# Score matmuls on 32-column tiles of the PE array, and 56 KB rows in the first two zero fills

## The chip, the cores and the metric

The kernel runs on one core of a Trainium2 chip. The metric is the device time of one execution in microseconds; for the kernel before, three timed runs gave 766.21, 766.40 and 766.55 us, median 766.4 us. Profiles come from one more execution, taken by the hardware profiler; its times are counted from the start of its span.

## The reference

A decode step with its gradients. Two tokens (B = 2, width D = 512) are layer-normalised; one branch is attention over the last 4,096 positions of a key and a value cache of 32,768 positions (8 KV heads of 128, 4 query heads each), the other is a two-layer squared-ReLU network whose output goes through silu and gates the first. The outputs are the result and the gradients of all inputs, the two caches among them.

```python
def _A_ref(x, k_cache, v_cache, wq, wo):
    W = min(4096, max(256, Sk // 4))
    k = jnp.repeat(k_cache[:, :, Sk - W:, :], rep, axis=1)
    v = jnp.repeat(v_cache[:, :, Sk - W:, :], rep, axis=1)
    scores = jnp.einsum("bhqd,bhkd->bhqk", q, k) * (Dh ** -0.5)
    p = _softmax(scores, axis=-1)
    o = jnp.einsum("bhqk,bhkd->bhqd", p, v)
    return ... @ wo
xn = _layernorm(x, axis=-1)
s = _A_ref(xn, A_k_cache, A_v_cache, A_wq, A_wo)
g = _silu(_B_ref(xn, B_w1, B_b1, B_w2, B_b2))
return x + s * g
_out, _vjp = jax.vjp(_f, A_x, A_k_cache, A_v_cache, A_wq, A_wo, B_w1, B_b1, B_w2, B_b2)
_grads = _vjp(grad_out)
```

The cache gradients, `out_2` (keys) and `out_3` (values), have the shape of the caches, 134 MB each in bf16. All but the last 4,096 of the 32,768 positions are zero, because the forward pass doesn't read them: 28,672 rows for each of 16 (batch, head) pairs of each cache have to be written with zeros, 7.34 MB (the profile's 7,168 KB) each and 234.9 MB in all.

## The kernel before

**Zero fills.** `zt` is a tile of zero bytes, 14,336 for each of 128 partitions (L80). `zf` (L90) issues a DMA from it to a stretch of `out_2` or `out_3` on the GpSimd queue (POOL); the 31 fills `qi` = 0 to 30 (L118 to L123) are issued one after the other at the head of the program, as far as the queue takes them. Fills in `zlong` (L107) are one DMA with 128 rows of 224 positions, 57,344 bytes (56 KB) each; fills in `zshort` (L108) are several DMAs with rows of up to 28 KB; the others, 0 and 1 among them, are one DMA with 2 x 128 rows of 112 positions, 28,672 bytes (28 KB) each. A row of 56 KB is written from the same 14,336 bytes of `zt`, which the DMA widens from bytes to 32-bit words (L96); the 28 KB rows are widened from bytes to bf16. The 32nd fill is the last DMA of SyncE's queue (SP), L641: it is issued after the store of `out_6` (L636) and after the fill before the last one on POOL has landed (L642).

**Loads.** SP's queue loads `w1`, `w2`, `wo`, `wq` and the first value block at once (L229 to L233). x, the incoming gradient and the two biases come on ScalarE's queue (ACT, L222 to L228); the bias `b2` is the last of these, and VectorE (DVE) converts it (L246) before anything else of the forward pass.

**Rounds.** Attention works in four rounds `r` (L430) of one batch and four KV heads. Heads are `NP` = 4 blocks of `RB` = 32 rows in every score tile of 128 x 512 in PSUM: row pr * 32 + g * 4 + i is head pr, position group g (of 8), query i (of 4). A round has a value block `vnat` and a key block `knat` of 128 x 16,384 bf16 (4,096 KB each). `scores` (L378) is called twice, for dP = dO V^T (`dp_ps`, from `vnat`) and S = Q K^T (`s_ps`, from `knat`). For each of 16 groups (2 halves x 8 g) it makes 8 transposes of 128 x 128 on TensorE (PE, L384) into one of two PSUM tiles `tp`, copies the result to one of four places of `tring` (three times on DVE, once on ACT, L387), and adds four matmuls (L391), one for each head, into `out_ps`. The stationary operand of these is a window of 128 columns in `zz`: zeros but for the 4 columns in which the queries of this head stand, so that each matmul adds zeros to the rows of all other heads and groups. Then come the softmax (L438 to L452), `contract` (L394) and `outer_store` (L412), which overwrites the block with its gradient and stores it on ACT's queue (L422). The next round's block is loaded on SP into the same buffer (L543, L550), which waits for that store.

**The end.** The last round holds the rest of the backward pass. Three rows of small results, `out_rows` (L499), `db2r` (L507) and `du_rows` (L515), are put into `zz`, which is no longer needed by then. After the rounds come the weight gradients: `out_4` from `wq` and `out_5` from `wo` on ACT's queue (L581, L587), `out_8` from `w2T` and `out_6` from `dw` on SP's (L610, L636), then the last fill.

The order of the instructions on each engine is set by a list scheduler with its own cost model; semaphores are set by dependences between tiles.

Of the kernel before, what the change touches and what calls it, by code (L numbers as in the profile page):

```python
# [11 lines left out]
BF16 = mybir.dt.bfloat16  # L12
# [4 lines left out]
def kernel(  # L17
# [24 lines left out]
    nc = tc.nc  # L42
    P = 128
    B, _, D = A_x.shape
# [3 lines left out]
    REP = HQ // HKV  # L48
# [5 lines left out]
    G = 8  # L54
    NP = 4
    PB = P // NP
    NCB = W // PB
    CC = NCB // G
    CH = 8
    NH = CC // CH  # L60
    RB = G * REP
    R = NP * RB
# [41 lines left out]
    ZQ = 2 * B * HKV  # L104
    zparts = [(out_2, q) for q in range(B * HKV)] + [(out_3, q) for q in range(B * HKV)]

    zlong = (3, 5, 7, 11, 12, 16, 17, 18, 19, 22, 23, 24, 25, 26, 27, 28, 29, 30)  # L107
    zshort = {  # L108
        2: ((5, 8, 2), (120, 68, 3), (128, 32, 1), (16, 1, 1)),
        4: ((3, 1, 2), (2, 99, 6), (128, 112, 1), (128, 102, 1), (86, 1, 1)),  # L110
# [60 lines left out]
    def pk_rows(t):  # L171
        return t.rearrange("b (p k) -> b k p", k=DK)
# [17 lines left out]
    nc.vector.tensor_scalar(out=nsel[:], in0=sel[:], scalar1=1e30, scalar2=-1e30, op0=ALU.mult, op1=ALU.add)  # L190
    pperm = const.tile([P, NP, PB], BF16, name="pperm")
    nc.vector.tensor_copy(out=pperm[:], in_=ident_bf[:].rearrange("p (k b) -> p b k", b=NP))
    ZO = R - REP
    ZW = NP * (ZO + R)
    zz = const.tile([P, 2 * ZW], BF16, name="zz")
    nc.vector.memset(zz[:], 0.0)
    zq = zz[:, 0:ZW].rearrange("p (n w) -> p n w", n=NP)
    zdo = zz[:, ZW:2 * ZW].rearrange("p (n w) -> p n w", n=NP)
    p_bf = const.tile([R, CC, PB, NP], BF16, name="p_bf")
# [20 lines left out]
    with tc.tile_pool(name="pw", bufs=1) as pw:  # L220
# [44 lines left out]
        for fk in range(FK):  # L265
            for k in range(DK):
                nc.tensor.matmul(hps[:, fk, :], lhsT=w1[:, k, fk:F:FK], rhs=xnT[:, k, :],
                                 start=(k == 0), stop=(k == DK - 1))
# [6 lines left out]
        for dk in range(DK):  # L275
            for fk in range(FK):
                nc.tensor.matmul(ups[:, dk, :], lhsT=w2[:, fk, dk:D:DK], rhs=h2T_bf[:, fk, :],
                                 start=(fk == 0), stop=(fk == FK - 1))
# [23 lines left out]
        for j0 in range(0, NJ, JG):  # L302
# [8 lines left out]
            for dk in range(DK):  # L311
                nc.tensor.matmul(dops[0:B, :, :], lhsT=dsT_bf[:, dk, :], rhs=woT[:, :, dk, :],
                                 start=(dk == 0), stop=(dk == DK - 1))
# [7 lines left out]
        for n0 in range(0, N, 512):  # L321
            qps = ps_o.tile([P, 512], F32, tag="o")
            for k in range(DK):
                nc.tensor.matmul(qps[0:B, :], lhsT=xnT[:, k, :], rhs=wq[:, k, n0:n0 + 512],
                                 start=(k == 0), stop=(k == DK - 1))
# [29 lines left out]
    small = attn.enter_context(tc.tile_pool(name="small", bufs=1))  # L355
    one = attn.enter_context(tc.tile_pool(name="one", bufs=1))
    epi = attn.enter_context(tc.tile_pool(name="epi", bufs=1))

    def group_sum(out_t, src, op, mask, comb, negate=False):
        tmp = small.tile([R, RB], F32, tag="gs")  # L360
        nc.vector.tensor_scalar(out=tmp[:], in0=mask[:].rearrange("p g i -> p (g i)"), scalar1=src[:, 0:1],
                                scalar2=None, op0=comb)
        nc.vector.tensor_reduce(out=out_t[:], in_=tmp[:], axis=AX.X, op=op, apply_transpose=True, negate=negate)
# [14 lines left out]
    def scores(out_ps, nat, zbuf):  # L378
        n = 0
        for half in range(NH):  # L380
            for g in range(G):
                tp = ps_t.tile([P, CH, P], BF16, tag="pt")
                for j in range(CH):
                    nc.tensor.transpose(tp[:, j, :], nat[:, g * CC + half * CH + j, :], pperm[:].rearrange("p b k -> p (b k)"))  # L384
                tF = tring[:, n % 4 * CH * R:(n % 4 + 1) * CH * R]
                tT = tF.rearrange("p (c b k) -> p c b k", c=CH, b=NP)
                evac(tF, tp[:].rearrange("p c k -> p (c k)"), eng=("act" if n % 4 == 3 else "dve"))  # L387
                n += 1
                for pr in range(NP):
                    o = ZO - (pr * RB + REP * g)  # L390
                    nc.tensor.matmul(out_ps[:, half * CH * PB:(half + 1) * CH * PB], lhsT=zbuf[:, pr, o:o + R], rhs=tT[:, :, pr, :],  # L391
                                     start=(g == 0 and pr == 0), stop=(g == G - 1 and pr == NP - 1))

    def contract(src, nat):  # L394
        cols = []
# [34 lines left out]
    for r in range(NR):  # L430
        nc.vector.tensor_copy(out=zdo[:, :, ZO:ZO + REP], in_=heads(doT_all, r))
        nc.vector.tensor_copy(out=zq[:, :, ZO:ZO + REP], in_=heads(qT_all, r))

# [33 lines left out]
        if r == NR - 1:  # L467
            o_rows = tring[0:B, 0:N]
            for h0 in range(0, HQ, 8):
                tp = ps_t.tile([B, 8, P], BF16, tag="pt")  # L470
                for h in range(8):
                    nc.tensor.transpose(tp[:, h, :], oT_all[:, h0 + h, :], ident_bf[:, :])
                evac(o_rows[:, h0 * DH:(h0 + 8) * DH], tp[:].rearrange("b h p -> b (h p)"))
            tp = ps_s.tile([P, NJ, B], BF16, tag="sd")
            for j in range(NJ):
                nc.tensor.transpose(tp[:, j, :], o_rows[:, j:N:NJ], ident_bf[0:B, 0:B])
            oT_alt = epi.tile([P, NJ, B], BF16, name="oT_alt")
            nc.vector.tensor_copy(out=oT_alt[:], in_=tp[:])
            sps = ps_s.tile([B, D], F32, tag="sd")
            for j in range(NJ):  # L480
                nc.tensor.matmul(sps[:], lhsT=oT_alt[:, j, :], rhs=wo[:, j, :], start=(j == 0), stop=(j == NJ - 1))
            s_rows = one.tile([B, D], F32, tag="e_sb")
            nc.vector.tensor_copy(out=s_rows[:], in_=sps[:])
            tp = ps_s.tile([P, DK, B], F32, tag="sd")
            for k in range(DK):
                nc.tensor.transpose(tp[:, k, :], s_rows[:, k:D:DK], ident_f[0:B, 0:B])
            acc_s = epi.tile([P, DK, B], F32, name="acc_s")
            nc.vector.tensor_copy(out=acc_s[:], in_=tp[:])

            outT = epi.tile([P, DK, B], F32, name="outT")  # L490
            nc.vector.tensor_tensor(out=outT[:], in0=acc_s[:], in1=gT[:], op=ALU.mult)
            nc.vector.tensor_tensor(out=outT[:], in0=outT[:], in1=xT_f[:], op=ALU.add)
            duT = epi.tile([P, DK, B], F32, name="duT")
            nc.vector.tensor_tensor(out=duT[:], in0=acc_s[:], in1=gsT[:], op=ALU.mult)
            duT_bf = epi.tile([P, DK, B], BF16, name="duT_bf")
            nc.vector.tensor_copy(out=duT_bf[:], in_=duT[:])

            tp = to_rows(outT, F32, ident_f[:, :], ps_s, "sd")
            out_rows = zz[0:B, 0:D]  # L499
            nc.vector.tensor_copy(out=pk_rows(out_rows), in_=tp[:])  # L500
            nc.sync.dma_start(out=out_0.rearrange("b s d -> (b s) d"), in_=out_rows)

            db2T = epi.tile([P, DK], F32, name="db2T")
            nc.vector.tensor_tensor(out=db2T[:], in0=duT[:, :, 0], in1=duT[:, :, 1], op=ALU.add)
            db2 = epi.tile([P, DK], BF16, name="db2")
            nc.vector.tensor_copy(out=db2[:], in_=db2T[:])
            db2r = zz[0:1, 2 * D:3 * D]  # L507
            tp1 = ps_s.tile([1, DK, P], BF16, tag="sd")
            for k in range(DK):
                nc.tensor.transpose(tp1[:, k, :], db2[:, k:k + 1], ident_bf[:, :])  # L510
            nc.vector.tensor_copy(out=db2r.rearrange("b (p k) -> b k p", k=DK), in_=tp1[:])
            nc.gpsimd.dma_start(out=out_9.rearrange("(b d) -> b d", b=1), in_=db2r)

            tp = to_rows(duT_bf, BF16, ident_bf[:, :], ps_s, "sd")
            du_rows = zz[0:B, D:2 * D]  # L515
            nc.vector.tensor_copy(out=pk_rows(du_rows), in_=tp[:])

            hps = ps_s.tile([P, FK, B], F32, tag="sd")
            for fk in range(FK):
                for dk in range(DK):  # L520
                    nc.tensor.matmul(hps[:, fk, :], lhsT=w2T[:, dk, fk * P:(fk + 1) * P], rhs=duT_bf[:, dk, :],
                                     start=(dk == 0), stop=(dk == DK - 1))
            dhBT = epi.tile([P, FK, B], F32, name="dhBT")
            nc.vector.scalar_tensor_tensor(out=dhBT[:], in0=hps[:], scalar=2.0, in1=rT[:], op0=ALU.mult, op1=ALU.mult)
            dhBT_bf = epi.tile([P, FK, B], BF16, name="dhBT_bf")
            nc.vector.tensor_copy(out=dhBT_bf[:], in_=dhBT[:])
            db1T = epi.tile([P, FK], F32, name="db1T")
            nc.vector.tensor_tensor(out=db1T[:], in0=dhBT[:, :, 0], in1=dhBT[:, :, 1], op=ALU.add)
            db1 = epi.tile([P, FK], BF16, name="db1")
            nc.vector.tensor_copy(out=db1[:], in_=db1T[:])  # L530
            nc.sync.dma_start(out=out_7.rearrange("(p j) -> p j", j=FK), in_=db1[:])

            xps = ps_s.tile([P, DK, B], F32, tag="sd")
            for k in range(DK):
                for fk in range(FK):
                    nc.tensor.matmul(xps[:, k, :], lhsT=w1T[:, fk, k * P:(k + 1) * P], rhs=dhBT_bf[:, fk, :],
                                     start=(fk == 0), stop=(fk == FK - 1))
            dxnT = epi.tile([P, DK, B], F32, name="dxnT")
            nc.vector.tensor_copy(out=dxnT[:], in_=xps[:])
# [13 lines left out]
        for hk in range(h0, h0 + NP) if b == B - 1 else ():  # L553
            xps = ps_m.tile([P, DK, B], F32, tag="m")
            for half in range(2):
# [7 lines left out]
                for k in range(DK):  # L563
                    for i in range(2):
                        nc.tensor.matmul(xps[:, k, :], lhsT=wqT[:, i, k, :], rhs=dqT_all[:, hk * REP + half * 2 + i, :],
                                         start=(half + k + i == 0), stop=(half == 1 and k == DK - 1 and i == 1))
# [105 lines left out]
```

## Time and profile before

| what | value |
|---|---|
| median of three runs | 766.4 us |
| the profiled execution's own time | 766.29 us |
| its span, first to last instruction | 764.5 us |
| PE / PE weight load / DVE / ACT busy | 399.7 / 261.8 / 275.8 / 214.5 us |
| HBM read / written | 45.62 / 280.50 MB |
| `scores` matmuls L391: dp_ps and s_ps | 256 each, mean 284 and 275 ns |
| `scores` transposes L384 | 1,024, mean 228 ns |

The page gives busy time of the engines as a share of the span, then the span in 40 slices of 19.1 us each, then the DMA queues: q0 is POOL's (the fills), q1 SP's, q10 ACT's. Matmuls are pipelined, so their mean durations add up to more than the time in which they ran: 16 of them in a row take 1.91 us in the timeline, not 16 x 0.28. The chain of waits at the bottom follows the last instruction of the compute engines back to the start; a DMA that is still on its way when all engines have ended isn't in it.

### The profile page before, as it was taken

Reading aid. Unit: us, or ns where it says so; the run is one execution under the profiler, and the core shown is the slowest. Engines: PE = TensorE matmul, PEld = TensorE weight load, DVE = VectorE, ACT = ScalarE, POOL = GpSimd, SP = SyncE. Lnnn points to the kernel's source line nnn. Section 1 sums busy time; section 2 is a strip of 40 time slices with the busy share of each in tenths; the row PEclk is TensorE's granted clock in tenths of the full one; section 3 lists DMA queues with packets and bytes.
Section 4 is the critical chain, followed back from the end, with each engine's and each line's share of the span. In section 5 each row is a group of like instructions: output and inputs, shape, how many; then the busy total and the mean of one; then the engine's idle time right before and its main releaser. Section 6 shows DMA issues by size and latency. Waiting matters only on the chain.

```text
span 764.5 us, 9399 instructions
## 1 busy us (share of the span) xinstructions
PE 399.7 (52%) x4118; PEld 261.8 (34%) x4118; DVE 275.8 (36%) x483; ACT 214.5 (28%) x313; POOL 35.1 (5%) x67
## 2 busy tenths in 40 slices
PE   0166774848503766870486683017645938759100
PEld 0153363734102654430275430016543424232000
DVE  3034252355501346450254653003343515567100
ACT  0034441145500124560122553002142307316100
POOL 3000010010000000000000000000000000000000
PEclk9998898968755995785599577559876957555555
DMA  9999999999999999999999999999999999999998
GB/s 360 433 425 427 442 422 430 438 426 425 429 428 438 427 446 430 413 427 435 435 427 440 427 433 438 420 433 429 437 430 436 430 440 430 418 438 425 436 417 379
DMA packets 12473, 326.73 MB, mean 427 GB/s; under 512 B 2898, under 2 KB 2906, under 8 KB 2934
## 3 DMA queue, kind: packets, MB, share of 16 engines
q0 software_dynamic: 8000, 227.55, 70.4%
q1 hardware_dynamic: 2696, 56.63, 19.3%
q10 hardware_dynamic: 1736, 41.95, 13.5%
q8 instruction: 32, 0.52, 0.3%
q14 instruction: 9, 0.07, 0.0%
HBM read 45.62 MB, written 280.50 MB: 427 GB/s over the span
## 4 chain that ended last, share of the span: by engine, by line
PE 33%; DMA 32%; DVE 14%; ACT 7%; issue 6%; ACTq 0%; DVEq 0%; SPq 0%
DMA out_dram<-nat 13%; DMA nat<-in_A_v_cache_dram 8%; DMA nat<-in_A_k_cache_dram 8%; PE ov L418 5%; PE s_ps L391 4%; PE tp L384 4%; DMA b_bf<-in_B_b_dram 4%; DVE tring L159 3%; PE dp_ps L391 2%; ACT p_bf L452 2%; ACT nat L157 2%; DVE ds_bf L465 2%; DVE nat L159 2%; PE wps L585 2%; PE ps L407 1%
## 5 line engine op out<-in xcount | busy, mean ns | idle before, releaser
L384 PE MATMUL tp<-pperm,nat 128*128 128x128 bf16 x1024 | 81.9, 228 | 136.4 <-DMA nat<-in_A_v_cache_dram 117.3
L159 DVE COPY tring<-tp 128x1024 bf16<-128x1024 bf16 (+1 forms) x98 | 65.5, 689 | 177.9 <-PE tp L384 168.3
L384 PEld LDWEIGHTS <-nat 128*128 128x128 bf16 x1024 | 70.8, 102 | 142.9 <-DMA nat<-in_A_v_cache_dram 119.3
L157 ACT CAST nat<-ov 128x512 bf16<-128x512 f32 x160 | 87.4, 590 | 61.9 <-PE ov L418 61.2
L157 ACT COPY tring<-tp 128x1024 bf16<-128x1024 bf16 (+1 forms) x34 | 34.4, 1011 | 239.7 <-PE tp L384 223.1
L159 DVE CAST nat<-ov 128x512 bf16<-128x512 f32 x96 | 65.7, 690 | 54.1 <-PE ov L418 51.4
L391 PEld LDWEIGHTS <-zz 128*128 128x128 bf16 x512 | 49.6, 100 | 37.3 <-issue 31.3
L101 POOL DMA_DIRECT2D out_dram<-zt x58 | 33.5, 581 | 529.3 <-DMA out_dram<-zt 526.1
L418 PE MATMUL ov<-bd,ds_bf 128*128 128x512 bf16 x128 | 49.2, 459 | 5.6 <-DVE nat L159 3.7
L418 PE MATMUL ov<-bd,p_bf 128*128 128x512 bf16 x128 | 48.6, 452 | 4.3 <-DVE nat L159 1.4
L391 PE MATMUL dp_ps<-tring,zz 128*128 128x256 bf16 x256 | 39.2, 284 | 12.1 <-DVE tring L159 6.9
L391 PE MATMUL s_ps<-tring,zz 128*128 128x256 bf16 x256 | 39.0, 275 | 10.9 <-DVE tring L159 9.9
L407 PE MATMUL ps<-t,nat 128*128 128x16 bf16 x1024 | 29.0, 174 | 13.7 <-DVE bd L372 6.8
L407 PEld LDWEIGHTS <-nat 128*128 128x128 bf16 x1024 | 28.9, 104 | 16.6 <-issue 11.4
L159 DVE CAST wq<-wps 128x512 bf16<-128x512 f32 x16 | 11.0, 690 | 42.4 <-PE wps L578 42.2
L399 PE MATMUL tp<-ident_bf,p_bf 128*128 128x128 bf16 x64 | 7.5, 312 | 34.9 <-ACT p_bf L452 34.9
L452 ACT ACTIVATE p_bf<-e_sb,rl 32x512 bf16<-32x512 f32 x16 | 22.8, 1424 | 3.4 <-DVE rl L449 3.3
L157 ACT CAST wq<-wps 128x512 bf16<-128x512 f32 x16 | 9.3, 586 | 50.6 <-PE wps L578 50.6
L465 DVE SCALAR_TENSOR_TENSOR ds_bf<-dp_ps,delta,p_bf 32x512 bf16<-32x512 f32 x16 | 21.8, 1360 | 0.2
L418 PEld LDWEIGHTS <-ds_bf 128*128 128x128 bf16 x128 | 12.9, 107 | 20.5 <-issue 18.2
L418 PEld LDWEIGHTS <-p_bf 128*128 128x128 bf16 x128 | 12.7, 108 | 19.5 <-issue 16.4
L399 PEld LDWEIGHTS <-p_bf 128*128 128x128 bf16 x64 | 6.5, 145 | 36.0 <-ACT p_bf L452 36.0
(195 smaller groups left out, 437.6 us busy)
## 6 DMA issues: line engine op xcount, KB each, us to landing
out_dram<-zt POOLq DMA_DIRECT2D x23, 7168.0 KB, 101.3
out_dram<-nat ACTq DMA_DIRECT2D x8, 4096.0 KB, 41.4
out_dram<-zt POOLq DMA_DIRECT2D x7, 3584.0 KB, 63.4
nat<-in_A_v_cache_dram SPq DMA_DIRECT2D x4, 4096.0 KB, 32.6
nat<-in_A_k_cache_dram SPq DMA_DIRECT2D x4, 4096.0 KB, 27.3
out_dram<-zt SPq DMA_DIRECT2D x1, 7168.0 KB, 52.2
out_dram<-zt POOLq DMA_DIRECT2D x2, 3488.0 KB, 64.6
out_dram<-zt POOLq DMA_DIRECT2D x1, 6120.0 KB, 85.8
```

The lines of the kernel that those rows point to most:

```text
L101: sw_fill.append(nc.gpsimd.dma_start(out=v, in_=zs))
L157: nc.scalar.copy(out=out_ap, in_=in_ap)
L159: nc.vector.tensor_copy(out=out_ap, in_=in_ap)
L384: nc.tensor.transpose(tp[:, j, :], nat[:, g * CC + half * CH + j, :], pperm[:].rearrange("p b k -> p (b k)"))
L391: nc.tensor.matmul(out_ps[:, half * CH * PB:(half + 1) * CH * PB], lhsT=zbuf[:, pr, o:o + R], rhs=tT[:, :, pr, :], start=(g == 0 and pr == ...
L399: nc.tensor.transpose(tp[:, cc, :], src[:, half * CH + cc].rearrange("r k b -> r (k b)"), ident_bf[:, :])
L407: nc.tensor.matmul(ps[:], lhsT=nat[:, g * CC + half * CH + cc, :], rhs=cols[half][:, cc, :, g, :], start=(half == 0 and g == 0 and cc == 0 ...
L418: nc.tensor.matmul(ov[:], lhsT=src[:, cc].rearrange("r k b -> r (k b)"), rhs=bd[:, gh * 4:(gh + 1) * 4, :], start=True, stop=True)
L452: nc.scalar.activation(out=p_bf[rb, :, :, pr], in_=e_sb[rb], func=ACT.Copy, scale=rl[rb, 0:1])
L465: nc.vector.scalar_tensor_tensor(out=ds_bf[rb, :, :, pr], in0=dp_c[rb], scalar=delta[rb, 0:1], in1=p_bf[rb, :, :, pr], op0=ALU.subtract, o ...
L585: nc.tensor.matmul(wps[:], lhsT=o_rows[:, j:N:NJ], rhs=ds_rows[:, :], start=True, stop=True)
```

## The change

`ZO` and `ZW` shrink: the window into `zz` is now 32 columns wide and no longer holds zeros for the other heads, and the four matmuls of a group write to 32 partitions each, `out_ps[pr * RB:(pr + 1) * RB, ...]`, which puts them on four different 32-column tiles of the PE array. Each head's rows now form an accumulation of their own, of 8 matmuls per half instead of 32 in one. The number of matmuls and transposes stays. Since `zz` is now 480 columns instead of 2,016, the three result rows get a tile of their own, `rows3`. Fills 0 and 1 become one DMA of 128 rows of 56 KB each.

```diff
-    zlong = (3, 5, 7, 11, 12, 16, 17, 18, 19, 22, 23, 24, 25, 26, 27, 28, 29, 30)
+    zlong = (0, 1, 3, 5, 7, 11, 12, 16, 17, 18, 19, 22, 23, 24, 25, 26, 27, 28, 29, 30)
...
-    ZO = R - REP
-    ZW = NP * (ZO + R)
+    ZO = RB - REP
+    ZW = NP * (ZO + RB)
...
+    rows3 = epi.tile([B, 3 * D], BF16, name="rows3")
...
                 for pr in range(NP):
-                    o = ZO - (pr * RB + REP * g)
-                    nc.tensor.matmul(out_ps[:, half * CH * PB:(half + 1) * CH * PB], lhsT=zbuf[:, pr, o:o + R], rhs=tT[:, :, pr, :],
-                                     start=(g == 0 and pr == 0), stop=(g == G - 1 and pr == NP - 1))
+                    o = ZO - REP * g
+                    nc.tensor.matmul(out_ps[pr * RB:(pr + 1) * RB, half * CH * PB:(half + 1) * CH * PB],
+                                     lhsT=zbuf[:, pr, o:o + RB], rhs=tT[:, :, pr, :], start=(g == 0), stop=(g == G - 1))
...
-            out_rows = zz[0:B, 0:D]
+            out_rows = rows3[0:B, 0:D]
...
-            db2r = zz[0:1, 2 * D:3 * D]
+            db2r = rows3[0:1, 2 * D:3 * D]
...
-            du_rows = zz[0:B, D:2 * D]
+            du_rows = rows3[0:B, D:2 * D]
```

In the order of the instructions, PE's queue keeps the same work with the same lag between a group's transposes and its matmuls; where the scheduler had cut two groups' transposes as 3 + 13 around four matmuls it now cuts them mostly as 8 + 8. DVE, ACT, POOL and SP keep their order but for a few neighbours that change places.

## The prediction

> **What bounds the kernel now.** I read the page's DMA part first, then what is still under way when the engines stop, then the start, then the score stages. Everything is counted for the profiled execution: 766.29 us, of which 764.5 are its span and 1.8 lie around it; the median of the runs, 766.4, is 0.1 above it.
>
> ```profile
> span 764.5 us, 9399 instructions
> ...
> DMA  9999999999999999999999999999999999999998
> GB/s 360 433 425 427 442 422 430 438 426 425 429 428 438 427 446 430 413 427 435 435 427 440 427 433 438 420 433 429 437 430 436 430 440 430 418 438 425 436 417 379
> DMA packets 12473, 326.73 MB, mean 427 GB/s; under 512 B 2898, under 2 KB 2906, under 8 KB 2934
> ## 3 DMA queue, kind: packets, MB, share of 16 engines
> q0 software_dynamic: 8000, 227.55, 70.4%
> q1 hardware_dynamic: 2696, 56.63, 19.3%
> q10 hardware_dynamic: 1736, 41.95, 13.5%
> ```
>
> The 16 DMA engines are over 90% busy in 39 of 40 slices, while PE is at 52%. The rate hardly depends on what is moved: about the mean 427 GB/s in slices full of loads, of stores, of fills alone. 326.73 MB at 427 GB/s is 765 us: the span is its bytes. The compute engines matter only if they leave the DMA engines without work. When they stop, there is a lot left:
>
> ```profile
> 710.84 0.33 SPq L636 DMA_DIRECT2D out_dram<-dw  x1
> 711.36 0.39 SPq L641 DMA_DIRECT2D out_dram<-zt  x1
> ```
>
> ```profile
> DMA packets 1134, 21.87 MB, mean 405 GB/s; under 512 B 128, under 2 KB 128, under 8 KB 128
> ## 3 DMA queue, kind: packets, MB, share of 16 engines
> q1 hardware_dynamic: 806, 10.87, 47.6%
> q0 software_dynamic: 165, 6.71, 28.9%
> q10 hardware_dynamic: 163, 4.29, 18.5%
> ```
>
> The first is SP's timeline, the second the DMA view of 711 to 765 us. SP issues its last DMA, the 32nd fill, at 711.36; it lands 52.2 us later. In between 21.87 MB go out, 6.71 of them POOL fills that wait for nothing. What must follow the last compute is `out_6` and the last fill, 1.84 + 7.34 = 9.18 MB or 21.5 us. So it would be enough to issue these at 764.5 - 0.9 - 21.5 = 742, less some 2 us from issue to first byte: the compute may end about 28 us later before the end moves, provided the other stores keep pace (if only the 6.71 MB of fills covered it, 16 us). I take 28 and keep 16. If it ends earlier, nothing is won: the same bytes remain.
>
> The start, and what PE does in the scores:
>
> ```profile
> 14.24 0.17 DVE L244 CAST b1T<-b_bf 128x14 f32<-128x14 bf16 x1 [5.64 <-DMA b_bf<-in_B_b_dram]
> 32.92 0.17 DVE L246 CAST b2T<-b_bf 128x4 f32<-128x4 bf16 x1 [18.50 <-DMA b_bf<-in_B_b_dram]
> ```
>
> ```profile
> 246.84 0.60 PE L391 MATMUL dp_ps<-tring,zz 128*128 128x256 bf16 x4
> 247.27 0.61 PE L384 MATMUL tp<-pperm,nat 128*128 128x128 bf16 x8
> 250.50 1.91 PE L391 MATMUL dp_ps<-tring,zz 128*128 128x256 bf16 x16
> ```
>
> The bias waits 18.5 us on a full DMA; nothing of the forward pass starts before. In the score stages matmuls follow at (1.91 - 0.28) / 15 = 0.11 us, so four cost 0.43 us and eight transposes 0.5 to 0.6. A call of 16 groups takes about 20 us (540.5 to 561 for the last key block), 1.25 us for a group, the rest of it copies of 0.69 (DVE) or 1.01 us (ACT) behind two `tp` buffers.
>
> **What the Trainium skill says.** "DMA: Bandwidth & Descriptors", section "Queues, rings and completion order": each DMA engine goes round the queues that have work, a packet from each. The trace agrees: from 20 to 68 us SP's 32 KB rows have 52.3% and the fills' 28 KB rows 48.5% of the engines, the ratio of the row lengths. The same page, "Where 436 GB/s comes from", puts the ceiling at 435 GB/s: with 427 in the mean there is 2% to win at most. "TensorEngine Tiling (Array Packing)", "Key Properties": tiles work independently, but a change of tiling mode drains TensorE. No run here shows either. "TensorE: Matmul & The Clock Gate", "Measured speedup vs the span model": three 32-column tiles ran 2.38 times as fast as one after the other.
>
> **The change part by part.**
>
> *56 KB rows in fills 0 and 1.* An engine has 427 / 16 = 26.7 GB/s, so a 28 KB row takes 1.07 us, a 56 KB row 2.15, a 32 KB load row 1.23 (estimates from the page's mean). The bytes stay. Fills beside loads moved at 428 GB/s (20 to 70 us), 56 KB rows beside stores at 429 (650 to 710), 56 KB rows alone at 433 (550 to 615). Bound for the 60 us concerned: -0.7 us if all of it went at 433, 0 at 428. I take 0. What moves is who is served: b2 has 8 rows for each engine, each behind one load row and one fill row: 8 x (1.07 + 1.23) = 18.4 us (measured 18.5), with 56 KB rows 8 x (2.15 + 1.23) = 27.0. With one or two rows of b1 that meet the fills too, the forward pass starts about 10 us late. The same holds for `wo`: by then 10 load rows have gone, 10 x 1.07 = 11 us. `wq` (landed at 57, first read at 84) has room for its 16 rows, 17 us, and so has the value block. So the first key load is issued at about 117 instead of 106.2 us.
>
> *Later meetings.* Fills go on as bytes allow, so a shift of the compute changes which fill a load or store meets. One that meets 56 KB rather than 28 KB rows takes 8 x 1.07 = 8.6 us longer: the value store issued at 185.50 had landed after 28.1 us (chain of waits), that at 446.99, among 56 KB rows, let the next value load go at 483.86, after 36.9. From none to three more of these on the chain: 0 to 26 us; I take 10.
>
> *Column tiles.* Four matmuls side by side instead of in a row: 0.43 us becomes 0.11 (all four at once) to 0.18 (at 2.38 times), so 0.25 to 0.32 us less for a group. Against it stand two changes of mode per group. A drain isn't in this trace; from above I take the part of a matmul's 0.28 us that pipelining hides, 0.17 us, from below 0. Best: -0.32 x 16 = -5 us a call; middle: -0.3 + 0.2 = -0.1, so -1.6 us a call; worst: no overlap and every matmul showing its whole 0.28 us, 4 x 0.28 - 0.43 + 2 x 0.17 = +1.0 us a group or +16 a call. Six calls lie on the chain (round 0 keys, both of rounds 1 and 2, round 3 keys): -30, -10 and +98 us.
>
> *The rest.* `rows3` and the smaller memset of `zz` (0.90 us, inside the wait for b2) cost nothing; weight loads of 32 columns are no longer than those of 128. If that cover were gone they'd be under 1 us.
>
> Sum for the end of compute: 711 + 10 + 10 - 10 = 721 us, 10 late, against 28 us of slack. The end is set by bytes: 764.5 in the span, 766.3 for the run.
>
> **The rivals.**
> *A, no change*, 766.3: as above. For it: the DMA row of nines, the 21.87 MB left. Against it: nothing but the drain, which no view shows.
> *B, slower through the tiles*: the drain eats the gain and PE falls behind until the fills run out. It decides from 28 us of delay on: with 10 from the start and 10 from meetings, 8 us remain, 8 / (6 x 16) = +0.08 us for a group; with early meetings as before, +0.19. At +0.4 a group: 711 + 10 + 17 + 38 = 776, and 776 + 2 + 21.5 + 0.9 = 800 in the span, 802 for the run. At the worst end 850 to 860. Against it: the skill's measured overlap, and copies, not matmuls, that fill over half of a group's time. Compute end over 740 would show it.
> *C, slightly slower, by rate*: other meetings of loads, stores and fills move 425 rather than 427 GB/s: 764.5 x 2 / 427 = +3.6 us, 769.9. For it: slices between 413 and 446. Against it: windows of every mixture at 428 to 433.
> *D, slightly faster*: 433 GB/s where the loads were, and the first 20 us (367 GB/s) somewhat better filled: -2 us, 764.3. Against it: loads fill the engines from 2 us on, so the first fill's start matters little.
>
> **How the numbers follow.** A 0.74, B 0.12, C 0.08, D 0.06. A measurement here can tell 0.2% (1.5 us) from no change. Predicted 766.3. A's own range is 765.2 to 767.7; with D's near side and C's whole I give 765.0 to 770.0 and leave out B and D's far end, some 16 in 100. Faster 0.06, within 0.2% 0.74, slower 0.20.
>
> **What would show it.** DMA row all nines and 427 GB/s again; b2's cast at 42 to 44 us; the first key load at 115 to 118; the wq load later by some 15 us; a score call of 15 to 19 us; SP's last issue anywhere between 690 and 740, with the end still near 764. It is wrong if the last issue lies beyond 740, if a DMA slice before the last is under 9, or if a score call takes over 21 us.

## The result, and the profile after

| | before | after |
|---|---|---|
| executions | 766.21 to 766.58 us (4) | 789.35, 791.53, 820.73, 825.60 us |
| ratio, 95% interval | | 1.031 [1.029, 1.034] |
| profiled execution, its span | 766.29, 764.5 us | 791.53, 789.8 us |

The change made the kernel slower by 3.1%. The ratio is that of the two executions near 790 us; that the others took some 30 us more belongs to the finding, for most kernels below that are slow are slow by several different amounts.

The page of the kernel after, its DMA part:

```profile
span 789.8 us, 9390 instructions
...
DMA  9999999999999999999999999999999999997089
GB/s 366 440 414 431 442 418 436 433 435 414 433 429 431 431 448 414 433 429 429 440 423 448 427 417 431 430 438 435 435 428 436 434 429 439 417 427 337 1 375 395
DMA packets 12218, 326.73 MB, mean 414 GB/s; under 512 B 2899, under 2 KB 2907, under 8 KB 2935
```

The bytes are the same to the last digit, and the rate where there is work is the same: the first 36 slices look like those of before. But slices 37 to 39 are no longer nines, and slice 38 is all but empty. The windows view over the end has, for each stretch, its length, the busy time of PE, PE's weight loads, DVE, ACT and POOL, then PE's clock, the busy share of the DMA engines and GB/s:

```profile
700.00:720.00 20.00, 14.88 (x97) 6.40 (x95) 10.77 (x23) 9.34 (x16) 0.00 (x0) 0.68 0.82 351
720.00:740.00 20.00, 10.82 (x49) 6.84 (x48) 12.94 (x15) 1.85 (x4) 0.00 (x0) 0.50 0.49 211
740.00:760.00 20.00, 18.39 (x41) 5.35 (x40) 14.49 (x22) 11.88 (x21) 0.00 (x0) 0.50 0.43 184
```

In these 60 us, (351 + 211 + 184) x 20 us = 14.9 MB moved. At 427 GB/s it would have been 25.6 MB. The missing 10.7 MB are 25 us of the engines' time, and the span is 789.8 - 764.5 = 25.3 us longer: this is the whole loss. The POOL fills ran out near 703 us, while the compute engines were still at work and their stores not yet issued. SP's timeline gives the end of the work:

```profile
765.90 0.33 SPq L637 DMA_DIRECT2D out_dram<-dw  x1
766.32 0.41 SPq L642 DMA_DIRECT2D out_dram<-zt  x1
```

The store of `out_6` is the first DMA after the last compute. It came at 710.84 before and comes at 765.90 now, 55.1 us later, and the last fill follows it at once in both. Only 23.5 us lie between that fill's issue and the end of the span, where there were 53. So some 30 us of delay were swallowed and 25 showed.

Where the 55 us arose is seen in DVE's timeline and in the chain of waits (start us, duration us, what):

```profile
20.50 0.17 DVE L244 CAST b1T<-b_bf 128x14 f32<-128x14 bf16 x1 [12.58 <-DMA b_bf<-in_B_b_dram]
46.50 0.17 DVE L246 CAST b2T<-b_bf 128x4 f32<-128x4 bf16 x1 [25.82 <-DMA b_bf<-in_B_b_dram]
```

```profile
119.86 29.77 DMA nat<-in_A_k_cache_dram
...
251.95 33.24 DMA nat<-in_A_k_cache_dram
...
389.02 49.56 DMA nat<-in_A_k_cache_dram
...
507.73 43.02 DMA out_dram<-nat
550.83 46.48 DMA nat<-in_A_k_cache_dram
```

The cast of `b2`, at which the forward pass begins, is 13.6 us late, and the first key load is issued at 119.86 instead of 106.18 us: it waits for the forward pass, because `w1` and `w2` stand in its buffer (L206) until they have been read and transposed (L343). Then the four key loads, from issue to landing, grow. With the first exponent of each round's softmax (ACT's timeline) as a mark:

| round | key load, before | after | exponent starts, before | after | late by |
|---|---|---|---|---|---|
| 0 | 27.9 us | 29.8 | 157.0 | 169.2 | 12.1 |
| 1 | 25.8 | 33.2 | 284.5 | 305.7 | 21.1 |
| 2 | 26.8 | 49.6 | 417.9 | 460.0 | 42.1 |
| 3 | 32.2 | 46.5 | 561.8 | 616.0 | 54.2 |

So 13.7 us come from the start and 41 from the rounds, most of it in front of rounds 2 and 3.

What a slow load consists of can be read from the DMA views of round 2's key load. First its size and time to landing, before and after; then the queues of the kernel after, from 389 to 426 us and from 426 to 438:

```profile
nat<-in_A_k_cache_dram SPq DMA_DIRECT2D x1, 4096.0 KB, 26.8
```

```profile
nat<-in_A_k_cache_dram SPq DMA_DIRECT2D x1, 4096.0 KB, 49.6
```

```profile
q0 software_dynamic: 397, 11.86, 75.7%
q1 hardware_dynamic: 163, 4.36, 55.7%
```

```profile
DMA packets 100, 4.99 MB, mean 416 GB/s; under 512 B 13, under 2 KB 13, under 8 KB 13
## 3 DMA queue, kind: packets, MB, share of 16 engines
q0 software_dynamic: 99, 4.99, 97.8%
q1 hardware_dynamic: 1, 0.00, 1.1%
```

q1 is SP's queue. By 426 us it had moved 4.36 MB, the load's 4.19 MB and the last rows of the value load before it. In the next 12 us it moved nothing, and the engines wrote fill rows alone; PE went on at 438.6. From the single packets in the trace, the load's 49.6 us divide into 6.9 from issue to its first row, 29.5 for its 128 rows, and 13.2 from the end of the last row to the landing. Before, the same load took 6.0 + 18.6 + 2.1 us. Round 3's took 8.3 + 25.0 + 13.2 after, and 5.1 + 19.1 + 8.0 before. So two things grow, each by about 11 us in round 2: the rows that share the engines with 56 KB rows, and a wait for completion after the last byte. That the 56 KB rows cause the second too is not shown; the last experiment below speaks against it. The wait agrees with a sentence of the Trainium skill, "DMA: Bandwidth & Descriptors", section "Queues, rings and completion order": the semaphore's increment is a strongly ordered write, which lands only after every earlier write of that DMA engine, those of its other queues among them. No run tried this apart.

The tiles do what they should. PE's timeline in round 2:

```profile
450.76 0.29 PE L392 MATMUL s_ps<-tring,zz 128*32 128x256 bf16 x4 [0.33 <-DVE tring L159]
450.98 0.62 PE L385 MATMUL tp<-pperm,nat 128*128 128x128 bf16 x8
```

Four matmuls together take as long as one, 0.29 us (0.60 before), and the transposes that follow start no later than before. From the landing of the key block to the exponent, the four rounds take 19.5, 20.5, 21.4 and 18.7 us instead of 23.0, 22.1, 21.6 and 21.4: 0.2 to 3.4 us less a call, 2.0 in the mean.

### The profile page after: what moved, and what is told of

Read it like the earlier page. It is cut to its first block, busy times and chain, and to the rows that moved or that the text cites. A ratio compares the mean times of both kernels' runs of the same rounds, so it can differ in the third digit from the quotient of the medians.

```text
span 789.8 us, 9390 instructions
## 1 busy us (share of the span) xinstructions
PE 387.6 (49%) x4109; PEld 235.2 (30%) x4118; DVE 275.9 (35%) x483; ACT 214.6 (27%) x313; POOL 34.7 (4%) x67
## 2 busy tenths in 40 slices
DMA packets 12218, 326.73 MB, mean 414 GB/s; under 512 B 2899, under 2 KB 2907, under 8 KB 2935
## 3 DMA queue, kind: packets, MB, share of 16 engines
q1 hardware_dynamic: 2696, 56.63, 22.1%
q10 hardware_dynamic: 1736, 41.95, 12.8%
## 4 chain that ended last, share of the span: by engine, by line
DMA 40%; PE 30%; DVE 12%; ACT 9%; issue 6%; ACTq 0%; DVEq 0%; SPq 0%
DMA nat<-in_A_k_cache_dram 20%; DMA out_dram<-nat 14%; PE ov L419 7%; DMA b_bf<-in_B_b_dram 6%; PE tp L385 4%; ACT nat L157 3%; ACT p_bf L453 2%; PE ps L408 2%; DVE nat L159 2%; PE s_ps L392 2%; DVE ds_bf L466 2%; PE wps L586 2%; ACT tring L157 2%; PE dops L312 1%; PE sps L482 1%
## 5 line engine op out<-in xcount | busy, mean ns | idle before, releaser
L385 PE MATMUL tp<-pperm,nat 128*128 128x128 bf16 x1024 | 94.8, 248 | 191.5 <-DMA nat<-in_A_v_cache_dram 124.6
L419 PE MATMUL ov<-bd,ds_bf 128*128 128x512 bf16 x124 | 47.1, 451 | 6.6 <-DVE nat L159 3.7
L408 PE MATMUL ps<-t,nat 128*128 128x16 bf16 x1024 | 28.5, 172 | 14.3 <-issue 7.4
L392 PEld LDWEIGHTS <-zz 128*32 128x32 bf16 x512 | 17.5, 97 | 36.1 <-issue 26.5
L392 PE MATMUL s_ps<-tring,zz 128*32 128x256 bf16 x256 | 20.3, 302 | 13.6 <-ACT tring L157 5.4
L392 PE MATMUL dp_ps<-tring,zz 128*32 128x256 bf16 x256 | 20.4, 325 | 7.2 <-ACT tring L157 4.3
L453 ACT ACTIVATE p_bf<-e_sb,rl 32x512 bf16<-32x512 f32 x16 | 22.8, 1423 | 3.4 <-DVE rl L450 3.3
L165 PE MATMUL pp<-xT_f,ones_f 128*128 128x2 f32 x8 | 1.9, 355 | 38.7 <-DVE goT L242 38.7
L419 PEld LDWEIGHTS <-ds_bf 128*128 128x128 bf16 x128 | 12.9, 107 | 20.5 <-issue 18.0
L419 PEld LDWEIGHTS <-p_bf 128*128 128x128 bf16 x128 | 12.9, 110 | 19.9 <-issue 17.2
```

Of the source, the lines that this page charges most:

```text
L392: nc.tensor.matmul(out_ps[pr * RB:(pr + 1) * RB, half * CH * PB:(half + 1) * CH * PB], lhsT=zbuf[:, pr, o:o + RB], rhs=tT[:, :, pr, :], st ...
L408: nc.tensor.matmul(ps[:], lhsT=nat[:, g * CC + half * CH + cc, :], rhs=cols[half][:, cc, :, g, :], start=(half == 0 and g == 0 and cc == 0 ...
L419: nc.tensor.matmul(ov[:], lhsT=src[:, cc].rearrange("r k b -> r (k b)"), rhs=bd[:, gh * 4:(gh + 1) * 4, :], start=True, stop=True)
L453: nc.scalar.activation(out=p_bf[rb, :, :, pr], in_=e_sb[rb], func=ACT.Copy, scale=rl[rb, 0:1])
```

## The experiments

Theories: *start and meetings*: fills 0 and 1 make the forward pass late, loads and stores then meet 56 KB rows, and each of these meetings makes the next one worse; *tiles*: the column tiles cost time somewhere; *start alone*: the late start is simply passed on. There is one profile of each kernel. Executions of the kernel before, measured beside each group of experiments, had a median of 766.5 to 766.6 us.

**One half each.** The tiles without the rows:

```diff
-    zlong = (0, 1, 3, 5, 7, 11, ...
+    zlong = (3, 5, 7, 11, ...
```

> The 32-column tiles alone, fills 0 and 1 with 28 KB rows as before. Theory R (the long rows in fills 0 and 1 make the start late, and late loads then meet the long fills 16, 17, 22 to 24): the first key load is issued at 106 us as before, a score call takes 16 us instead of 20, SP's last issue comes between 685 and 705 us, the DMA engines never run out, 766 us. Rival T (the tiles slow PE down, by drains or by a lower granted clock): last issue later than before's 711 us, time over 775 us.

Twelve executions took 766.30 to 766.75 us, ratio 1.000 [0.999, 1.001]. The rows without the tiles are the kernel before with the same line changed the other way:

> The kernel before with 56 KB rows in fills 0 and 1, and its own 128-column matmuls. Theory R: the first key load is issued at about 120 us, loads of the later rounds meet long fills, SP's last issue lies 55 to 85 us after 711 us (the change's 55 us, plus up to six calls of 3.5 us that are no longer saved), 790 to 830 us. Rival T: 766 us, because the tiles are away.

One of four took 766.16 us like the kernel before, three took 832.1 to 835.4; the profile is of the second kind, span 830.3 us, `b2` cast at 46.33, last issue at 806.91. The loss is the rows', and *tiles* falls: alone they cost nothing, and without them the loss is no smaller. That they gain nothing was expected, but not where SP's last issues lie with the tiles alone:

```profile
709.28 0.33 SPq L637 DMA_DIRECT2D out_dram<-dw  x1
713.36 0.39 SPq L642 DMA_DIRECT2D out_dram<-zt  x1
```

The last fill was expected at 685 to 705 and came at 713. It isn't held by the compute here: `out_6` had been issued 4 us before, and what it waits for then is the landing of the last POOL fill but one. So from here on the issue of `out_6` is taken as the end of the compute; both coincide in the slow kernels, and by chance in the kernel before. At 709.28 that is 1.6 us earlier than before, far less than six calls of 2 us. The first key load takes 33.8 us here instead of 27.9, and its exponent comes 5.9 us later than before; by round 3 it comes 2.3 us earlier (559.5 against 561.8).

**Long rows only where they aren't met.** The kernel after, with fills 16, 17 and 22 to 24 in 28 KB rows:

```diff
-    zlong = (0, 1, 3, 5, 7, 11, 12, 16, 17, 18, 19, 22, 23, 24, 25, ...
+    zlong = (0, 1, 3, 5, 7, 11, 12, 18, 19, 25, ...
```

> The changed kernel, but fills 16, 17, 22, 23 and 24, which the loads and stores of rounds 2 and 3 met, have 28 KB rows. Theory R: the start is as late as in the changed kernel (first key load at 120 us), but the round 2 key load takes about 30 us instead of 49.6 and that of round 3 about 32 instead of 46.5, SP's last issue comes before 735 us and the time is back at 766 us. If the late start were enough by itself, or the tiles were the cause, it would stay over 785 us.

Twelve executions, 765.86 to 766.53 us, ratio 0.9996 [0.999, 1.000]. Round 2's key load in the DMA view, where the kernel after has 49.6 us:

```profile
nat<-in_A_k_cache_dram SPq DMA_DIRECT2D x1, 4096.0 KB, 25.4
```

Its parts are now 5.5 + 18.4 + 1.4 us. The late start is still there (`b2` cast at 42.41, first key load at 117.33), and yet `out_6` is issued at 690.45, 20 us earlier than before, none of which shows in the time: *start alone* has a gap. But this start is 2.5 us earlier than that of the kernel after, and the load of round 2 is issued at 372.4 instead of 389.0. By the bytes of POOL's queue it falls into fills 14 and 15 and doesn't reach 16 and 17; in the kernel before, issued at 369.5, it took 26.8 us. So this profile doesn't show what shorter rows in fills 16 and 17 save. What the run shows is in the times: of its twelve executions none was slow, of the kernel after, with the same head, all four.

The opposite: tiles, an early start, and long rows in three more of the fills that are met:

```diff
-    zlong = (0, 1, 3, 5, 7, 11, 12, 16, ...
+    zlong = (3, 5, 7, 9, 11, 12, 14, 16, 17, 18, 19, 21, 22, ...
```

> The tiles, a start with 28 KB rows in fills 0 and 1 as before, but fills 9, 14 and 21, which the loads and stores of rounds 1 to 3 meet, have 56 KB rows. Theory M: the start is on time (first key load at 106 to 109 us), yet each load and store that meets them takes 35 to 50 us instead of 25 to 33, the feedback sets in, SP's last issue lies beyond 745 us and the time is over 780 us. If only the start mattered, it would stay at 766 us.

Four executions, 803.89 to 804.49 us, ratio 1.049 [1.048, 1.051], last issue at 778.69. Its chain of waits:

```profile
108.38 33.73 DMA nat<-in_A_k_cache_dram
...
388.45 49.93 DMA nat<-in_A_k_cache_dram
...
488.29 42.29 DMA out_dram<-nat
...
562.37 46.44 DMA nat<-in_A_k_cache_dram
```

The start is early (108), and from round 2 on the waits are those of the kernel after: 49.9 of them divides into 6.0 + 29.8 + 14.1. So long rows that are met are enough by themselves. With none at all (tiles, `zlong = ()`):

> The tiles, and no fill has rows over 28 KB. Theory M (a load or store costs by the length of the fill rows it meets): no load takes over 33 us, no store over 33, SP's last issue 20 to 45 us before 711 us, and the time 766 us, since the bytes bound it. If it is faster than 766 us, long rows cost something by themselves; if slower, short rows do.

Twelve executions, 766.86 to 767.35 us, ratio 1.0007 [1.000, 1.002]; no key load takes over 30.5 us. SP's last issue was expected 20 to 45 us before 711:

```profile
673.74 0.33 SPq L637 DMA_DIRECT2D out_dram<-dw  x1
730.34 0.39 SPq L642 DMA_DIRECT2D out_dram<-zt  x1
```

The fill misses that, because it waits 56 us for the last POOL fill but one; the compute, 37 us earlier than before, has it, and the time doesn't change. A wait for completion isn't tied to long rows alone: round 2's key load here divides into 6.0 + 16.3 + 8.2 us.

**The late start without the long rows at the head.** Two attempts to move `b2` behind `wo` on SP's queue, with short rows (first) and with those of the change (second):

```diff
-        dma_store.dma_start(out=b2_bf[:], in_=B_b2.rearrange(...))
...
+        dma_load.dma_start(out=b2_bf[:], in_=B_b2.rearrange(...))
```

> The tiles with 28 KB rows in fills 0 and 1, but the load of the second bias is put on SP's queue behind wo, so that the forward pass starts late without any long row: b2 at about 46 us, first key load at about 119 us. Theory R, with the late start as the only thing that the long rows do: as the changed kernel, the key loads of rounds 2 and 3 meet the long fills, last issue at 745 to 800 us, time 780 us or more. If the long rows harm in another way (rate, other loads late), it stays at 766 us.

> The changed kernel with its long first rows, but the second bias is loaded on SP's queue behind wo, and DVE's conversion of it stands behind the layer norm instead of ahead of it. Theory S (the late start is what the long rows do; from there on a feedback through long fills decides): the first key load is issued before 115 us instead of 119.9, the key load of round 2 takes under 33 us, SP's last issue before 735 us, 766 us in all executions. Rival W (the long rows harm in another way, or the start gains nothing because wo or the first bias is late too): first key load at 117 us or later, and at least some executions over 785 us.

The first took 766.05 to 766.53 us (twelve), ratio 0.9997 [0.999, 1.001], but it isn't the experiment that was meant. Its DVE timeline:

```profile
16.49 0.16 DVE L166 TENSOR_SCALAR meanb<-pp 128x2 f32<-128x2 f32 x1 [1.96 <-PE pp L165]
...
48.98 0.17 DVE L246 CAST b2T<-b_bf 128x4 f32<-128x4 bf16 x1 [22.73 <-DMA b_bf<-in_B_b_dram]
```

The scheduler put the layer norm ahead of the cast, so most of the forward pass no longer waited for `b2`, and the first key load was issued at 108.79. The second took 766.33, 791.99, 805.1 and 812.8 us, profiled span 790.2. Its start isn't earlier (first key load at 121.61), because `wo` is as late as `b2`; from the costliest groups of its page:

```profile
L308 PE MATMUL tp<-ident_bf,wo 128*128 128x128 bf16 x128 | 13.7, 289 | 26.5 <-DMA wo<-in_A_wo_dram 24.6
```

Next, DVE operations that multiply a tile of zeros (`ds_bf`) by a number of the forward pass, put into the forward pass ahead of the rows of dO, behind which the first key load comes; they leave the output as it is. With 16 of them, and with 32, in the kernel with the tiles alone:

```diff
+        dsz = ds_bf[:].rearrange("r c k b -> r (c k b)")
+        for _ in range(16):
+            nc.vector.tensor_scalar(out=dsz, in0=dsz, scalar1=gsT[:, 0, 0:1], scalar2=None, op0=ALU.mult)
```

> The tiles with 28 KB rows in fills 0 and 1, and 16 DVE operations put into the chain before the output-gradient rows, which multiply a tile of zeros by a number and leave it zero: they only make the forward pass late, by 10 to 17 us (0.6 to 1.1 us each). Theory S: a late start alone is enough, without any long row at the start; first key load at 116 to 125 us, later loads meet fills 11 and 16, 17, at least some executions over 785 us. Rival W: the start is late, but the loads keep their short fills, 766 us in all executions.

> As the late start with short rows, but 32 operations on the tile of zeros instead of 16, so that the first key load is issued at 122 to 132 us, beyond the 117.3 us at which executions still ran through and the 119.9 us at which they did not. Theory S2 (there is a tipping point: the first key load has to be through before fill 5, whose 56 KB rows start at about 136 us): that load lands after 148 us, the key loads of rounds 2 and 3 take 45 us and more, at least most executions over 780 us. Rival W (only long rows at the head of the program do the harm): 766 us.

Ratios 0.9999 [0.999, 1.001] and 1.0001 [0.999, 1.001] (twelve each). An operation took 0.76 us, and the first key load was issued at 115.75 and 118.41 us: earlier than both had been meant to be, and not yet as late as in the kernel after. It still landed at 141.9 and 143.2, where it had landed at 142.0 after an issue at 108.3. Up to here lateness costs nothing.

Two changes to the head of the fills instead: in the kernel after, fill 5 short, and fill 0 short:

```diff
-    zlong = (0, 1, 3, 5, 7, ...
+    zlong = (0, 1, 3, 7, ...
```

```diff
-    zlong = (0, 1, 3, 5, 7, ...
+    zlong = (1, 3, 5, 7, ...
```

> The changed kernel with 28 KB rows in fill 5 alone. Theory S2: the start is as late as in the changed kernel (first key load at 117 to 122 us), but that load lands before 148 us and later loads keep their short fills: SP's last issue before 742 us, 766 us in all executions. If fill 5 is not the tipping point, some executions stay over 785 us.

> The changed kernel with 28 KB rows in fill 0 and 56 KB rows in fill 1. The second bias and wo are through before fill 1 begins at about 42 us, so theory S2 expects the start on time: first key load at 106 to 110 us, 766 us in all executions. If long rows at the head harm by way of wq or the first value block, the first key load is at 115 us or later, and some executions are over 785 us.

With fill 5 short, 17 of 20 executions took 765.86 to 766.90 us and three 771.9 to 775.9, ratio 1.001 [1.000, 1.003]; the profile, of the first kind, has the first key load issued at 117.59 and landed at 141.8. The three miss what was expected, and the profile's start is one at which a kernel with a long fill 5 ran through too (117.33 above), so fill 5 is a part of the edge at most. With fill 0 short, all twelve took 766.04 to 766.91 us, ratio 0.9999 [0.999, 1.001], and `b2` was cast at 33.69. So it is fill 0's rows that set it off; fill 1's alone do no harm.

**Past the edge.** Nine heavier DVE operations on the same tile of zeros, 2.34 us each, behind the copy of the queries (`qT_all`), in the kernel with the tiles alone:

```diff
+        qd = pw.tile([P, 1], F32, name="qd")
+        nc.vector.tensor_copy(out=qd[:], in_=qT_all[:, 0, 0:1])
+        dsz = ds_bf[:].rearrange("r c k b -> r (c k b)")
+        for _ in range(9):
+            nc.vector.scalar_tensor_tensor(out=dsz, in0=dsz, scalar=qd[:, 0:1], in1=dsz, op0=ALU.mult, op1=ALU.mult)
```

> The tiles with 28 KB rows in fills 0 and 1, and nine DVE operations of about 2 us among the copies that the first key load waits for (they multiply a tile of zeros, which stays zero). First key load at 119 to 128 us. Theory S2 (only the time of the first key load matters, whatever made it late): that load ends among the 56 KB rows of fill 5, the key loads of rounds 2 and 3 take 38 to 50 us, last issue at 742 us or later, most executions at 772 us or more. Rival W (the long rows at the head themselves are needed): 766 us in all executions.

Five executions: 789.32, 791.26, 794.34, 795.01 and 823.26 us, ratio 1.035 [1.033, 1.038] (of the first four). The chain of waits of the profiled one, 823.26 us long, and the DMA row of its page:

```profile
125.66 29.93 DMA nat<-in_A_k_cache_dram
...
256.10 46.65 DMA nat<-in_A_k_cache_dram
...
422.27 49.78 DMA nat<-in_A_k_cache_dram
...
594.05 48.46 DMA nat<-in_A_k_cache_dram
```

```profile
DMA  9999999999999999999999999999999999157089
```

Fills 0 and 1 have the rows of before here, and `b2` is early; only DVE is late. The times, the long loads and the hole at the end are those of the change, two kinds of execution some 30 us apart included. So a late start past the edge is enough, without long rows in fills 0 and 1. Whether it would cost anything with no long rows at all wasn't tried. The same with fill 5 short:

> The same late start, with 28 KB rows in fill 5. Theory S2: the first key load lands some 5 us or more earlier after its issue than in the other kernel of this pair, last issue before 742 us in most executions, 766 us, or at most 776 us where the later fills are still met. Rival W: no difference from the other kernel of this pair.

Of 20 executions 10 took 766.19 to 767.02 us, five 774.33 to 777.81 and five 792.70 to 794.23; median 770.67; the ratio of the fourteen up to 776 us is 1.003 [1.001, 1.005]. The five over 790 us go beyond the 776 that had been allowed. The chain of a profile of the middle kind, span 773.3 us:

```profile
122.97 27.29 DMA nat<-in_A_k_cache_dram
...
252.32 25.23 DMA nat<-in_A_k_cache_dram
...
382.71 48.66 DMA nat<-in_A_k_cache_dram
...
537.32 43.29 DMA nat<-in_A_k_cache_dram
```

The first two key loads are now as short as before; the long ones of rounds 2 and 3 remain. So the late start loses in half of the executions without a long fill 5 too. Last, the kernel after with fills 16 and 17 alone made short:

> The changed kernel with 28 KB rows in fills 16 and 17, which the key load of round 2 met. Theory F (each late meeting makes the next one): with this load at about 30 us instead of 49.6, round 3 starts some 20 us earlier, and the last issue lies at 730 to 750 us: 766 to 775 us at most. If the meetings add up without one making the next, fills 22 to 24 still cost 25 us and the time stays over 780 us in some executions.

775.67, 775.70, 776.34 and 804.87 us, ratio 1.012 [1.010, 1.014] (of the first three); last issue at 750.47. The chain of waits:

```profile
391.55 38.91 DMA nat<-in_A_k_cache_dram
...
499.62 37.92 DMA out_dram<-nat
537.62 42.28 DMA nat<-in_A_k_cache_dram
```

Round 2's key load takes 38.9 us instead of 49.6 and is through 8.1 us earlier, though issued 2.5 us later. The store ahead of round 3's load then takes 5.1 us less (37.9 against 43.0) and that load 4.2 less, so that it is through 17.4 us earlier; of these, 15.9 are left at the last issue. With the meeting in round 2, part of those that follow goes, as *start and meetings* has it; but the four times agree with it only in part, for three lie just above the 775 expected and one over 780.

This run also parts the two costs of round 2. At nearly the same place as in the kernel after, the load meets 28 KB rows and, but for one, no 56 KB rows, and divides into 5.5 + 20.6 + 12.8 us. So shorter rows take 8.9 us from its rows and next to nothing from its wait for completion. What makes that wait long isn't shown. The trace has one clue: a load counts as landed at the sixteenth increment of its semaphore, and fifteen of the sixteen had come by 419.2 us here, the last at 430.5. In the kernel with the late DVE start and fill 5 short, fifteen of round 2's had come by 406.3, the last at 431.4; in the kernel before, fifteen of round 3's by 529.8, the last at 540.4. A single laggard decides there; in round 2 of the kernel after, twelve came late together, between 436.4 and 438.6.

The kernels in the order of their first key load, one profile each:

| kernel | first key load issued, landed | `out_6` issued | span |
|---|---|---|---|
| before | 106.2, 134.1 | 710.8 | 764.5 |
| fill 0 short | 107.1, 134.3 | 698.3 | 764.9 |
| tiles only | 108.3, 142.0 | 709.3 | 764.7 |
| more long rows that are met | 108.4, 142.1 | 778.3 | 802.1 |
| tiles, `b2` moved | 108.8, 140.9 | 700.0 | 764.7 |
| no long rows | 109.8, 135.9 | 673.7 | 765.3 |
| 16 small operations | 115.8, 141.9 | 700.1 | 764.5 |
| short where met | 117.3, 142.4 | 690.5 | 764.5 |
| fill 5 short | 117.6, 141.8 | 697.7 | 764.6 |
| 32 small operations | 118.4, 143.2 | 701.5 | 764.6 |
| fills 16, 17 short | 119.1, 150.1 | 750.1 | 773.9 |
| after | 119.9, 149.6 | 765.9 | 789.8 |
| rows, `b2` moved | 121.6, 155.4 | 766.4 | 790.2 |
| rows only | 122.2, 155.4 | 806.5 | 830.3 |
| past the edge, fill 5 short | 123.0, 150.3 | 749.5 | 773.3 |
| past the edge | 125.7, 155.6 | 797.6 | 821.5 |

Two edges stand out. First, in all kernels that have fills with long rows, issues from 108 to 118.4 us all land at 141 to 143; from 119.1 on the landing jumps to 150 and more. (There is such a jump already between 107.1 and 108.3, from 134 to 142, and it costs nothing.) The packets show how: in the kernel with 32 small operations 120 of the load's 128 rows had ended by 138.0 and the last at 141.7; in the kernel after 120 had ended by 139.9, but the 124th ended at 142.2, the 126th at 144.4 and the last at 149.0, among fill 5's 56 KB rows. Here too it is one laggard: fifteen of the sixteen increments had come by 143.0. Why it is late isn't seen in the trace. With fill 5 short, an issue at 123.0 lands at 150.3 too, but there the whole load is late (120 rows by 147.2). Second, in the seven slow profiles of the table the span ends 23.8 to 23.9 us after the issue of `out_6`. That decides from 764.5 - 23.8 = 740.7 us on; in the kernels that take 766 or 767 us `out_6` is issued between 674 and 711, and its place doesn't show in their times.

That one kernel has executions of 766, 775, 790 and 820 us follows from this if its start lies near the first edge and differs a little from one execution to the next: `b2` was cast at 42.41 and at 46.50 in two kernels with the same head. `b2` isn't all of it, for with a cast at 42.52 the first key load was issued at 119.1 (fills 16, 17 short). This is argued; an execution that isn't profiled leaves no trace.

## Why the prediction was wrong

- *The bytes and the rate*: right. 326.73 MB again, nines up to slice 36, 56 KB rows no slower in the mean. Two readings beside it were loose. The shares of 52.3% and 48.5% stand as 1.08 to 1, the row lengths as 1.14 to 1; the wait for `b2`, 18.5 us against 18.4 estimated, is the better sign that the queues take turns by rows. And single slices of the profile before reach 446 GB/s, above the 435 taken as the ceiling.
- *The slack*: right. It was put at about 28 us; measured it is 740.7 - 710.8 = 30. The compute could end anywhere from 674 to 711 without a trace in the time, and the slow spans point to 740.7 as the edge. By this edge, the 721 of the prediction's sum would have left the time as before.
- *The start*: `b2` 8 x (2.15 + 1.23) = 27.0 us, measured wait 25.8. First key load at "about 117", measured 119.9 in this profile and 117.3, 117.6 and 119.1 in others with the same head. Right in mechanism, 3 us short here: `b1` was cast 6.3 us later, where one or two rows, 1 to 2 us, had been allowed. These 3 us lie on both sides of the edge.
- *Column tiles*: taken at -1.6 us a call, measured -2.0 in the mean of four, with no cost of a drain to be seen, and no effect on the end. Weight loads of 32 columns took 97 ns, those of 128 columns before 100 ns, as assumed.
- *Later meetings*: **this step failed.** "From none to three more of these on the chain: 0 to 26 us; I take 10." The rounds took 41 us, net of what the tiles saved. Three parts of the term were too small. The price: a meeting was put at 8.6 us, eight more rows of 28 KB; round 2's key load took 22.8 us longer, 10.9 in its rows, 11.1 in the completion, which wasn't in the sum at all, and 0.9 until its first row. Short rows in fills 16 and 17 take 8.9 us of the rows away, so the price of long rows was near the mark; the wait for completion stays at 12.8 us without them, and its cause is open. The number: not three meetings at most but each of the four key loads, which took 1.9, 7.4, 22.8 and 14.3 us longer, 46 in all; the stores ahead of those of rounds 1 to 3 added 2.6 together, and the calls won back 8, which makes the 41. And the independence: a late load makes the next load and store late, which puts them among the long rows of fills 11, 16, 17 and 22 to 24; the sum treated each as a chance of its own. Round 2's 49.6 us fall to 38.9 when only the rows that it meets are short, and what follows it shortens too; adding long rows to an early start gives 804 us.
- *The rivals*: B had the place and the threshold (the compute ends past 740) and a time between the two kinds of execution, 802, but for the tiles, which the run with the tiles alone clears. Its reckoning of the 28 us, "with 10 from the start and 10 from meetings, 8 us remain", was the right path, with 10 where 41 came. What the prediction named as a proof against itself, a last issue beyond 740, is what came.

No version ran faster than the kernel before beyond its interval: as long as the bytes set the end there is nothing to gain from earlier compute. The best of the combinations is as fast as before.

## What to carry to other kernels

A kernel bound by its DMA bytes is only safe from its compute chain as long as the chain's slack isn't used up, so price what a small delay grows to along the chain, not only the delay. Where loads on the chain share the DMA engines with filler traffic, price each load with the rows that it would meet if it came 10 us later, and with its completion, and keep the long rows for stretches in which no load of the chain can fall. If executions of one kernel fall into groups, look for a place where a transfer is near such an edge before comparing means.

## What the runs showed of the hardware that had not been expected

- The wait from a load's last row to its landing isn't constant: 0.4 to 5.0 us for most key loads, 10.6 to 15.9 us in rounds 2 and 3 of all profiles over 780 us, and up to 17.4 (round 2, past the edge with fill 5 short). It isn't bound to 56 KB rows: among rows of 28 KB (and a single one of 56 KB at most) it took 8.0 us in round 3 of the kernel before, 9.1 there with the tiles alone, 8.2 in round 2 without any long rows, and 12.8 in round 2 with fills 16 and 17 short.
- From issue to its first row a key load took 4.8 to 9.2 us in all kernels; what grows most is what follows.
- Four 32-column matmuls that go to four column tiles took 0.29 us together. The 1,024 transposes between them took 248 ns in the mean instead of 228, and yet the calls became shorter by 2.0 us in the mean, so a cost of the change of tiling mode can't be told apart in these traces.
